# The leftover queries of a batch pair: a feed-forward block of their own instead of a shared block of three tiles

## The chip, the cores and the metric

The kernel runs on one core of one Trainium2 chip, in one launch. The metric is device time in microseconds (us), the median of several executions. A profile is one further execution taken by the hardware profiler; its times are compared with its own execution's time.

The engines are named as in the profile: PE (TensorE, matmuls; PEld its weight loads), DVE (VectorE), ACT (ScalarE), POOL (GpSimd), SP (SyncE, which issues most DMAs).

## The reference

All of attention is float32; the feed-forward weights come as float64.

```
# B, H, S, D = 8, 8, 576, 64
scores = q @ k.T / sqrt(D)                       # per batch and head: 576 x 576
kth    = 32nd largest of each row
scores = where(scores >= kth, scores, -1e9)
attn   = softmax(scores) ; a = attn @ v          # (B, H, S, D)
x      = a.transpose(0, 2, 1, 3).reshape(4608, 512)
h      = x @ w_in                                # 512 -> 2048
g      = where(h > 0, h, exp(min(h, 0)) - 1)     # ELU
out    = g @ w_out                               # 2048 -> 512
```

## The kernel before

**Attention in steps.** The 576 queries of a batch are four tiles of 128 and a rest of 64. A step is one query tile with two heads; a rest step takes 64 queries with four heads, so that it too fills 128 rows. Batches are worked through in pairs, 36 steps a pair, 144 in all. In an even batch the order is tiles (0, 1), tiles (2, 3), rest; in an odd batch it is rest, (4, 5), (6, 7), where 4 to 7 are the odd batch's four tiles. The rests of both batches of a pair lie next to each other and make up one tile of 128 tokens, number 8, which the code calls `rest`. In the first batch of all, tiles go singly.

A step runs through all engines: `scores` multiplies queries and keys on PE (`scps`, line 331), and ACT copies the scaled scores to `sc` (339); `select` finds the 32 largest of each row on DVE, in four rounds of MAX8 and three of MATCH_REPLACE8 for each of two rows of 576; `mask` makes masked exponentials and their sums on ACT (407, 408); `normalise` divides on POOL (418 to 425); `turn` transposes the attention nine times 128x128 on PE (`eps`, 444) and copies it to `et` on ACT (445); `attend` multiplies by the values (`avps`, 470), for two steps at a time where tiles go in twos, and `finish` copies the result to the block's `xT` (497).

**Feed-forward in blocks.** Tiles of tokens are gathered in blocks. When all tiles of a block have their attention, `finish` puts the block's pieces at the end of the list `ffn`. A block has 16 pieces `hidden(f)`, four matmuls each with as many columns as the block has tokens (`hps`, 545), and four pieces `project(s, part)` for each of its tiles, four matmuls each of 512 columns (`ops`, 573). Each float32 matmul of these stands in the profile as two records. After `hidden` ACT takes two Relus (555, 558) out of PSUM whenever a PSUM bank's share is full, `bank = dm // n_tok` pieces: every four pieces for one tile, every two for two tiles, every one for three. Then it takes an exponential (560) and mostly a subtraction of one (564) over `unit = max(2, bank)` pieces; the two halves of the ELU are added on POOL (515) or DVE (517). `project` waits for that sum, and its result goes through `osb` (582) to the output by SP's queue (585).

Pair 0 has the blocks (0), (1), (2), (3), (8), (4, 5), (6, 7). The others have (0, 1), (2, 3), (8, 4, 5), (6, 7). A block of one tile takes its `xT` from `xpool` (three buffers of 128 tokens); a larger one from the pool `xt` (two buffers of `T` tokens). `T` also sizes the buffers of `g` and `n`.

**Who goes when.** After the first eight steps every engine's order is written out by the Python loop (`manual_schedule`). In iteration n it emits `scores` of step n + 2, `attend` of what is closed, `select` of step n in four parts, `mask` of n - 1, `turn` of n - 2 and `normalise` of n - 1, and between them four calls of `feed`. These hand out feed-forward pieces by costs in units of the table `HIDDEN` (per `hidden` piece, by tiles in the block) and `PROJECT`. Each block has a place in the list `due`: the step count at which it is ready, and the cost of all blocks that are ready before it.

```
tiles[qt].block.ready = n + 1.0 if n <= tight else n + 2.5
...
due.append((blk.ready, total))
total += NF * HIDDEN[blk.slots] + 4 * blk.slots * PROJECT
...
ahead = [(w - fed["sum"]) / (x - fed["at"]) for x, w in due if x > fed["at"]]
if ahead:
    fed["over"] += max(0.0, share * min(ahead))
```

So the rate at any time is the smallest over all blocks still to come of (work that must go before the block) / (steps until it is ready). A piece is given out while half its cost is covered by what has gathered in `over`. What is left when the loop ends is emitted in one go, the last pair's block (6, 7) above all.

Of the kernel before, what the change touches and what calls it, by code (L numbers as in the profile page):

```python
# [17 lines left out]
TAKEN = -1.0e30  # L18
EPS = 1.0e-9
STEEP = 2.0**96  # L20
HIDDEN = {1: 1.1, 2: 1.85, 3: 2.7}
PROJECT = 3.55


# [57 lines left out]
def kernel(  # L82
# [10 lines left out]
    P = nc.NUM_PARTITIONS  # L93
# [7 lines left out]
    NC = dm // P  # L101
    NF = dff // P
    NG = NF // 2
    T = 3 * P
    KEYS, QUERIES = R, R + S
    Q = 32
    NB = S // Q
# [383 lines left out]
    def finish(blk, parts, at, cols, src):  # L491
        if blk.xT is None:
            if blk.slots == 1:
                blk.xT = xpool.tile([P, NC, P], FP32, tag="xT", name="xT")
            else:
                blk.xT = late["x"].tile([P, NC, T], FP32, tag="xT", name="xT")
        nc.scalar.copy(blk.xT[:, at, cols], src)
# [23 lines left out]
    def ffn_pieces(blk):  # L521
# [4 lines left out]
        def hidden(f):  # L526
# [3 lines left out]
            elif f % NG == 0 and blk.number > 0:  # L530
                g = late["g"].tile([P, NG, T], FP32, tag="g", name="gT")
                blk.gT.append(g[:])
            if f % unit == 0:
# [4 lines left out]
                else:  # L538
                    n = late["f"].tile([P, 2 * T], FP32, tag="n", name="n")
                blk.n = n[:, 0 : unit * n_tok].rearrange("p (f t) -> p f t", f=unit)  # L540
# [45 lines left out]

        part = HIDDEN[blk.slots]
        behind = 2 * NF if blk.number else 0
# [13 lines left out]
    for b in range(B):  # L602
        if b % 2 == 0:
            rest = 2 * J
            division = [(0,), (1,), (2,), (3,), (rest,), (4, 5), (6, 7)]
            if b > 0:
                division = [(0, 1), (2, 3), (rest, 4, 5), (6, 7)]
            slots = {}
            for part in division:
                blk = Block(len(blocks), len(part))  # L610
                blocks.append(blk)
                slots.update((x, (blk, s)) for s, x in enumerate(part))
        first[b] = len(steps)
        tiles = []
        for qt in range(J + 1):
            r0 = b * S + (JP if qt == J else qt if b == 0 else qt * P)
            if qt == J:
                (blk, slot), c0, n = slots[rest], (b % 2) * R, R
                rows = slice(r0, r0 + R)
            else:  # L620
                (blk, slot), c0, n = slots[(b % 2) * J + qt], 0, P
                rows = slice(r0, r0 + J * (P - 1) + 1, J) if b == 0 else slice(r0, r0 + P)
            c0 += slot * P
            t = Tile(b, qt, rows, blk, slice(c0, c0 + n))
            blk.left += NHP
            blk.tiles[slot].append(t)
            tiles.append(t)
        order = [(0, 1), (2, 3), (J,)] if b % 2 == 0 else [(J,), (0, 1), (2, 3)]
        if b == 0:
            order[:2] = [(0,), (1,), (2,), (3,)]  # L630
        for qts in order:
            for hp in range(NHP // 2 if qts == (J,) else NHP):
                group = Group([tiles[qt] for qt in qts], hp)
                steps += [Step(tiles[qt], hp, group, i) for i, qt in enumerate(qts)]
            for qt in qts:
                n = len(steps)
                tiles[qt].block.ready = n + 1.0 if n <= tight else n + 2.5
    NS = len(steps)
    total = 0.0
    for blk in sorted(blocks, key=lambda x: x.ready):  # L640
        due.append((blk.ready, total))
        total += NF * HIDDEN[blk.slots] + 4 * blk.slots * PROJECT

# [57 lines left out]
    main, rest, other = slice(0, J), slice(J, J + 1), slice(J + 1, 2 * J + 1)  # L701
# [90 lines left out]
```

## Time and profile before

| what | value |
|---|---|
| time, median of three runs | 1645.8 us (1644.03 to 1645.95) |
| the profiled execution: time, span | 1642.57 us, 1640.8 us |
| mean granted TensorE clock | 0.974 |
| PE busy | 1581.7 us, 96% |
| DVE busy | 1453.4 us, 89% |
| ACT busy | 1187.7 us, 72% |
| POOL busy | 708.7 us, 43% |
| `hps` matmul records of 128, 256, 384 columns | 640, 1408, 384 |
| `ops` matmul records of 512 columns | 1152 |

The span is the time from the first instruction to the last. Busy shares are means over stages: in the first 200 us weights are converted and the clock is partly low, then attention and feed-forward run together, and after some 1520 us selection on DVE is over and feed-forward work remains. A matmul's busy time includes its way through the array, which overlaps the next one, so the price of a matmul in a row of equals is the distance from start to start, not its duration. For the same reason an idle time shown for PE is less than what was lost.

### The profile page before, as it was taken

How to read it: one execution, taken by the hardware profiler on the slowest of the kernel's cores; microseconds unless marked ns; L12 is line 12 of the kernel's file. 1: busy time of each engine (PE TensorE's matmuls, PEld its weight loads, DVE VectorE, ACT ScalarE, POOL GpSimd, SP SyncE). 2: the span in 40 equal slices, each digit the busy share in tenths (PEclk: the TensorE clock that was granted, in tenths of full speed). 3: DMA queues.
4: the chain of work that ended last, by engine and by line, in shares of the span. 5: the costliest groups of instructions: out<-in, count | busy, mean ns of one | idle time of the engine just before them, and what ended most of it. 6: DMA issues, size and time to landing. Idle time of an engine off the chain costs nothing.

```text
span 1640.8 us, 25344 instructions
## 1 busy us (share of the span) xinstructions
PE 1581.7 (96%) x8276; PEld 1011.8 (62%) x8276; DVE 1453.4 (89%) x2981; ACT 1187.7 (72%) x2400; POOL 708.7 (43%) x1534
## 2 busy tenths in 40 slices
PE   4788999999999999999999999999999999999999
PEld 3566777666575757555566666655557575755564
DVE  6987999999999999999999699999999599998000
ACT  6887778778695867778678686868759595958521
POOL 4775445445353534445335353535435353534300
PEclk8579999999999999999999999999999999999999
DMA  7431221012100310012100211012100201000000
GB/s 226 151 128 25 50 40 26 7 22 45 42 1 7 59 42 8 7 22 44 36 14 15 43 30 28 1 28 44 36 14 0 43 1 35 1 13 2 7 13 14
DMA packets 188037, 56.18 MB, mean 34 GB/s; under 512 B 178177, under 2 KB 179201, under 8 KB 187905
## 3 DMA queue, kind: packets, MB, share of 16 engines
q1 hardware_dynamic: 186704, 54.26, 14.1%
q8 instruction: 66, 1.08, 0.3%
q14 instruction: 67, 0.54, 0.1%
q10 hardware_dynamic: 1200, 0.30, 0.1%
HBM read 45.09 MB, written 9.44 MB: 33 GB/s over the span
## 4 chain that ended last, share of the span: by engine, by line
PE 76%; ACT 12%; DVE 7%; POOL 3%; issue 1%; DMA 1%; SPq 0%; ACTq 0%; DVEq 0%; POOLq 0%
PE ops L573 29%; PE hps L545 23%; PE avps L470 10%; PE scps L331 7%; PE eps L444 6%; DVE wk L378 3%; DVE m L385 3%; ACT sc L408 2%; ACT et L445 2%; ACT sc L407 2%; DVE m L373 1%; ACT n L564 1%; ACT n L555 1%; ACT sc L339 1%; ACT n L560 1%
## 5 line engine op out<-in xcount | busy, mean ns | idle before, releaser
L385 DVE MAX8 m<-wk 128x8 f32<-128x576 f32 x816 | 577.9, 752 | 0.3 <-POOL den L406 0.3
L545 PE MATMUL hps<-xT,w_in 128*128 128x256 f32 (+2 forms) x2432 | 545.8, 374 | 0.0
L573 PE MATMUL ops<-w_out,gT 128*128 128x512 f32 x1152 | 523.6, 599 | 0.0
L545 PEld LDWEIGHTS hps<-xT,w_in 128*128 128x128 f32 x2432 | 406.0, 192 | 100.1 <-issue 26.3
L378 DVE MATCH_REPLACE8 wk<-m,wk 128x576 f32<-128x576 f32 x544 | 401.4, 748 | 0.0
L573 PEld LDWEIGHTS ops<-w_out,gT 128*128 128x128 f32 x1152 | 209.0, 190 | 233.9 <-issue 232.8
L418 POOL TENSOR_SCALAR dene<-den 128x2 f32<-128x2 f32 x144 | 32.9, 228 | 686.5 <-ACT sc L408 686.1
L408 ACT ACTIVATE sc<-sc,den 128x576 f32<-128x576 f32 x288 | 223.6, 776 | 65.5 <-POOL den L406 44.2
L407 ACT ACTIVATE sc<-sc,m 128x576 f32<-128x576 f32 x288 | 225.3, 782 | 10.8 <-DVE m L385 10.7
L470 PE MATMUL avps<-et,vT 128*64 128x256 f32 (+2 forms) x2080 | 207.2, 330 | 17.4 <-ACT et L445 17.2
L425 POOL TENSOR_SCALAR sc<-sc,rec 128x576 f32<-128x576 f32 x288 | 213.0, 750 | 15.0 <-POOL rec L423 0.2
L331 PE MATMUL scps<-kqT 64*128 64x288 f32 (+1 forms) x1280 | 206.0, 442 | 13.6 <-ACT kqT L307 9.1
L339 ACT ACTIVATE sc<-scps 128x576 f32<-128x576 f32 x288 | 171.8, 647 | 65.1 <-PE scps L331 65.1
L445 ACT COPY et<-eps 128x512 f32<-128x512 f32 x288 | 164.6, 571 | 73.4 <-PE eps L444 73.4
L378 DVE MATCH_REPLACE8 wk<-m,sc 128x576 f32<-128x576 f32 x272 | 200.6, 748 | 0.0
L373 DVE MAX8 m<-sc 128x8 f32<-128x576 f32 x272 | 191.6, 749 | 8.8 <-ACT sc L339 8.8
L444 PEld LDWEIGHTS eps<-ident,sc 128*128 128x128 f32 x1152 | 144.9, 144 | 87.2 <-issue 52.7
L444 PE MATMUL eps<-ident,sc 128*128 128x128 f32 x1152 | 177.1, 279 | 13.7 <-POOL sc L425 13.7
L470 PEld LDWEIGHTS avps<-et,vT 128*64 128x64 f32 x2080 | 128.5, 142 | 98.8 <-ACT et L445 31.7
L515 POOL TENSOR_TENSOR gT<-n,gT 128x512 f32<-128x512 f32 (+1 forms) x119 | 164.9, 1386 | 31.2 <-ACT n L564 31.1
L331 PEld LDWEIGHTS scps<-kqT 64*128 64x128 f32 (+1 forms) x1280 | 111.3, 182 | 89.5 <-issue 43.8
L555 ACT ACTIVATE n<-hps 128x512 f32<-128x512 f32 (+1 forms) x156 | 87.3, 559 | 56.8 <-PE hps L545 56.0
(53 smaller groups left out, 1089.6 us busy)
## 6 DMA issues: line engine op xcount, KB each, us to landing
raw<-in_moe_w_in_dram SPq DMA_DIRECT2D x16, 512.0 KB, 6.1
vT<-in_v_dram SPq DMA_DIRECT2D x64, 128.0 KB, 2.5
raw<-in_moe_w_out_dram SPq DMA_DIRECT2D x16, 512.0 KB, 3.6
out_dram<-osb SPq DMA_DIRECT2D x32, 256.0 KB, 2.1
kin<-in_k_dram SPq DMA_DIRECT2D x112, 72.0 KB, 2.5
qin<-in_q_dram SPq DMA_DIRECT2D x112, 72.0 KB, 2.6
kin<-in_k_dram SPq DMA_DIRECT2D x8, 128.0 KB, 4.5
vT<-in_v_dram SPq DMA_DIRECT2D x64, 16.0 KB, 2.2
```

The lines of the kernel that those rows point to most:

```text
L331: nc.tensor.matmul(wide[i][rows, half, 0:HS], kq[part, q0 : q0 + u.t.ql], kq[part, k0 : k0 + HS], start=True, stop=True,)
L373: nc.vector.max(found[i], cur[i])
L378: nc.vector.match_replace(wk[i], found[i], cur[i], TAKEN)
L385: nc.vector.max(found[i], cur[i])
L407: nc.scalar.activation(sc, sc, AF.Prelu, scale=-1.0, bias=low, alpha=1.0 / STEEP)
L408: nc.scalar.activation(sc, sc, AF.Exp, scale=-STEEP, bias=gap, accum_out=u.den[:, i : i + 1])
L425: nc.gpsimd.tensor_scalar(u.sc[:, i, :], u.sc[:, i, :], rec[:, i : i + 1], 1.0, ALU.mult, ALU.mult)
L444: nc.tensor.transpose(ps[:, c * P : (c + 1) * P], sc[:, c0 : c0 + P], ident[:])
L445: nc.scalar.copy(g.et[:, chunks, u.at, :], ps[:, 0 : n * P].rearrange("p (c q) -> p c q", c=n),)
L470: nc.tensor.matmul(ps[i * D : (i + 1) * D, cols], vt[:, 2 * J + i if c == J else i * J + c, :], w, start=(c == 0), stop=(c == J),)
L545: nc.tensor.matmul(blk.h[:, f % bank, :], w_in[:, i, f * P : (f + 1) * P], blk.xT[:, i, 0:n_tok], start=(i == 0), stop=(i == NC - 1),)
L573: nc.tensor.matmul(blk.o[:], blk.gT[f // NG][:, f % NG, s * P : (s + 1) * P], w_out[:, f, :], start=(f == 0), stop=(f == NF - 1),)
```

## The change

The tile of leftover queries (`rest`, number 8) is a block by itself in all pairs, as it was in pair 0; (4, 5) is then a block of two. Three-tile blocks no longer occur, so their entry in `HIDDEN` goes, and `T`, the largest block's tokens, becomes 256. A pair after the first has five blocks instead of four, and all blocks together cost 1066.4 units by the table instead of 1054.4.

```diff
-HIDDEN = {1: 1.1, 2: 1.85, 3: 2.7}
+HIDDEN = {1: 1.1, 2: 1.85}
...
-    T = 3 * P
+    T = 2 * P
...
             division = [(0,), (1,), (2,), (3,), (rest,), (4, 5), (6, 7)]
             if b > 0:
-                division = [(0, 1), (2, 3), (rest, 4, 5), (6, 7)]
+                division = [(0, 1), (2, 3), (rest,), (4, 5), (6, 7)]
```

`due` and the pieces follow from `division`; no other line differs.

## The prediction

> **What bounds the kernel now.** I read the page's busy times and slices first, then busy time by stretch, then TensorE's waits, then its timeline, since the change touches nearly only matmuls.
>
> ```profile
> PE 1581.7 (96%) x8276; PEld 1011.8 (62%) x8276; DVE 1453.4 (89%) x2981; ACT 1187.7 (72%) x2400; POOL 708.7 (43%) x1534
> PE   4788999999999999999999999999999999999999
> DVE  6987999999999999999999699999999599998000
> PEclk8579999999999999999999999999999999999999
> ```
>
> PE and DVE are both full to slice 35; then DVE stops and PE alone goes on. The page cannot say which is late, so I ask for stretches (PE's busy time is the second figure, DVE's the fourth):
>
> ```profile
> 350.00:560.00 210.00, 206.49 (x1041) 135.26 (x1040) 210.00 (x432) 159.44 (x323) 93.36 (x213) 1.00 0.15 30
> 560.00:780.00 220.00, 215.84 (x1145) 133.68 (x1144) 220.00 (x453) 169.63 (x345) 100.62 (x223) 1.00 0.14 27
> 780.00:990.00 210.00, 210.00 (x1084) 131.66 (x1083) 195.77 (x405) 151.57 (x306) 88.89 (x207) 1.00 0.14 28
> ```
>
> From 350 to 780 us DVE never stops and PE idles 3.5 + 4.2 = 7.7 us; from 780 on PE never stops and DVE has to wait. Up to 780 DVE sets the pace, after it PE. PE's waits of 350 to 780 us are nearly one kind, a context matmul that waits for ScalarE's copy of the turned attention (total, times, longest):
>
> ```profile
> PE avps L470 <- ACT et L445: 6.1, 10, 1.2
> ```
>
> These idle times are too small, since matmul ends are modelled. Start to start in the timeline, an undisturbed context group takes 839.74 - 837.43 = 2.31 us, and one that waits 549.31 - 545.83 = 3.48: it lost 1.17 us where the row shows 0.53.
>
> ```profile
> 545.83 0.65 PE L470 MATMUL avps<-et,vT 128*64 128x256 f32 x2
> 547.01 2.37 PE L470 MATMUL avps<-et,vT 128*64 128x256 f32 x18 [0.53 <-ACT et L445]
> 549.31 3.72 PE L545 MATMUL hps<-xT,w_in 128*128 128x256 f32 x16
> ...
> 837.43 2.38 PE L470 MATMUL avps<-et,vT 128*64 128x256 f32 x20
> 839.74 3.70 PE L573 MATMUL ops<-w_out,gT 128*128 128x512 f32 x8
> ```
>
> **The new matmuls.** `hidden` has 64 matmuls a block, two records each. Three pairs have a block of three tiles, so 3 x 128 = 384 records of 384 columns become 384 of 128 and 384 of 256. Their price is the pitch, first start to next group's start:
>
> ```profile
> 262.15 1.06 PE L545 MATMUL hps<-xT,w_in 128*128 128x128 f32 x8
> 263.04 0.60 PE L444 MATMUL eps<-ident,sc 128*128 128x128 f32 x4
> ...
> 843.82 1.89 PE L545 MATMUL hps<-xT,w_in 128*128 128x256 f32 x8
> 845.55 0.60 PE L444 MATMUL eps<-ident,sc 128*128 128x128 f32 x4
> ...
> 1475.40 2.75 PE L545 MATMUL hps<-xT,w_in 128*128 128x384 f32 x8
> 1478.07 1.24 PE L331 MATMUL scps<-kqT 64*128 64x288 f32 x8
> ```
>
> 0.89 / 8 = 111 ns for 128 columns, 1.73 / 8 = 216 for 256. The third, 2.67 / 8 = 334, ends at a score matmul; such a change costs about 0.09 us once (the same form ahead of a transpose, at 1487.63, takes 2.58 / 8 = 323). So 111 + 216 - 323 = 4 ns, at most 5: 384 x 5 = **+1.9 us** on PE. Groups of 16 to 24 at 128 columns reach 117 ns; that end gives 384 x 10 = 3.8 us. `project` keeps its 576 matmuls.
>
> A page states another price. The Trainium skill, "TensorE: Matmul & The Clock Gate", section "Back-to-back issue gap", says that in a stream of weight loads and matmuls 128 columns take about 81 ns and 512 about 131, so a quarter of the columns is far more than a quarter of the time; it speaks against this change. As an estimate from that page, 81/131 of this trace's 429 ns for 512 columns would be 265 ns, the sum would grow by 384 x 154 ns = 59 us, and the kernel would be slower. The 111 ns above contradict it here, and I go by the row.
>
> ScalarE has 32 outputs of 384 columns (0.485 us) and 16 of 768 (0.845) per block, 29.0 us; now 24 of 512 (0.592) and 24 of 512 (0.632), 29.4. GpSimd's eight sums of 768 (1.82) become twelve of 512 (1.28): 14.6 to 15.3. Both lie beside PE (ACT 72%, POOL 43%) and I take nothing; if their cover were gone they would cost 0.4 and 0.7 us a pair. SyncE's loads and stores are the same number; stores move and nobody waits for them. `xpool` gives the single block its own xT, which removes a claim on the two wide ones; no wait on those shows.
>
> **What moves.** This is the larger part. `feed` gives out feed-forward work at the smallest rate at which, for each block, all earlier blocks are done when it is ready. Units come from HIDDEN and PROJECT: two tiles 58.0, one 31.8, three 85.8. Pairs have 36 steps. Following the `due` list:
> - before: block (4,5) of pair 0 is ready at step 30.5 with 159.0 units ahead; the three-tile blocks at 66.5, 102.5, 138.5 with 391.0, 650.8, 910.6; the last at 146.5 with 996.4. The rates are 232/36 = 6.44 units a step to 66.5, 519.6/72 = 7.22 to 138.5, 85.8/8 = 10.7 to the end.
> - after: the single block is ready at 58.5, so three tiles no longer wait for 66.5. The rates are 7.25 to 54.5 (174/24) and about 7.34 from there to the end (675.4/92).
>
> So work leaves the last eight steps and goes to steps 30 to 66, those in which PE idles. The two programs' instruction orders say the same: TensorE's is identical until about step 30; priced by the pitches, the new one has placed 7 us more PE work by step 36, 14 by 44, 22 by 56, keeps a lead of 25 to 30, and gives it back from step 137 (14 at 140, 5 at 143).
>
> **What it is worth.** One unit is (27.6 + 27.6) / 58.0 = 0.95 us, from the last block in the timeline:
>
> ```profile
> 1581.64 27.79 PE L545 MATMUL hps<-xT,w_in 128*128 128x256 f32 x128
> 1609.27 27.63 PE L573 MATMUL ops<-w_out,gT 128*128 128x512 f32 x64
> ```
>
> Counting nine turning transposes a step, PE in full stretches makes 40 steps from the first turning transpose of step 80 (885.5 us) to that of step 120 (1306.4), 10.52 a step: 7.22 x 0.95 = 6.86 feed-forward and 3.66 attention. At 6.44 units a step would be 6.12 + 3.66 = 9.78, close to DVE's 9.64 (a selection every 9.64 us where it is full). Measured from step 36 (431.3) to 64 (714.6): 283.3 / 28 = 10.12. So 0.34 us a step is lost, about 12 us over the 36 steps; doubling the 7.7 us of idle by the example above gives 15. I take 12. At 7.25 units PE needs 6.89 + 3.66 = 10.55, falls 0.9 us a step behind DVE, and after three steps always has work. Those first steps still wait (about 2 us): **-10 us**. Later, attention waits where the three-tile block begins with nothing left to give out, as at 1491.92: that row's group takes 3.70 instead of 2.31 us. Three of those become ordinary places, but more blocks begin just in time: **-1 us**, with 0 and -3 as ends.
>
> The end is covered: before, step 143 is turned on PE at 1567.1, 57 us after its selection begins at 1510; some 20 is the least that the chain of mask, scaling and turning took (steps 16 to 24). With 10.5 against 9.64 us a step from the last place where DVE is held up, a delay near 26 us grows to about 40, still over 20. So what is late next is PE itself.
>
> Sum: 1.9 - 10 - 1 = **-9 us**. The profiled execution took 1642.57 (span 1640.8 and 1.8 around it) and would take 1633.5; it lies 3.2 us under the median of the runs, 1645.8, so the forecast is **1637**.
>
> **Rivals.**
> - Waits only move (0.13). In the new order the first steps of each odd batch, when DVE has just been held up, carry `hidden` and not `project`; ScalarE then has 6.3 us of attention and 4 x 1.2 us of outputs against PE's 10.5. If twelve context groups there pay 0.8 us each as at 545.83 or less, 9.6 of the 11 go: +0.5, 1646. For it: PE's waits are all on ScalarE. Against: at 858 us the same pattern takes 2.32 us, undisturbed.
> - Slower (0.10): ScalarE falls behind in every `hidden` phase. Some 14 phases follow step 36, each with two context groups; at 1.2 us each (545.83) that is 34 us, where 12 + 3 are lost now, so with 1.9 it is +21 at worst. It decides from 15 + 3.3 - 1.9 = 16.4 us, 0.6 us a group. At 879.09 the second group of a full phase takes 2.84, 0.53 more; the first none, so 0.27 on average.
> - Columns priced by weight loading: to end 3.3 us slower the new matmuls would have to cost 11 + 3.3 - 1.9 = 12.4 us more, 12.4 / 384 = 32 ns above 111. No row after 200 us shows it (0.03).
> - The work moves but gives little because step 30 to 66 lost less than worked out (only the 7.7 shown as idle, 2 of it kept): -5, 1641 (0.14). The change doing nothing is excluded by the order.
>
> **How the numbers follow.** Forecast 0.60; its own range, from 1.9 - 13 - 3 (15 lost, 2 kept) to 3.8 - 8 (12 lost, 4 kept, nothing later), is -14 to -4. The 0.2% that can be told from no change is 3.3 us. Faster by more: 0.60 + 0.14 = 0.74; same: the first rival, 0.13; slower: 0.10 + 0.03 = 0.13. The range runs from -14 to just under the first rival's end, with the -5 case inside: 1631 to 1645; the two slower cases stay out.
>
> **What would show it.** PE's idle time between 350 and 780 us should fall from 7.7 to under 3; DVE should wait more there; the 128-column rows of `hidden` should go from 640 to 1024 records at 111 to 117 ns; PE's last eight steps should take 10.5 us each, DVE end later than 1520, PE's tail shrink. Wrong if TensorE's waits on `et` stay above 10 in number there, or the tail shows idle PE before the last block.

## The result, and the profile after

| | median of runs | profiled execution, span |
|---|---|---|
| before | 1645.1 us (1644.0 to 1646.0, 4 runs) | 1642.57, 1640.8 us |
| after | 1667.9 us (1664.2 to 1668.9, 4 runs) | 1667.47, 1665.7 us |

The changed kernel is slower: ratio 1.0135, 95% interval 1.0117 to 1.0152, some 22 us. The forecast was 1637, faster.

The page of after, the busy times and DVE's slices:

```profile
PE 1584.3 (95%) x8660; PEld 1054.9 (63%) x8660; DVE 1454.5 (87%) x2981; ACT 1191.5 (72%) x2400; POOL 713.1 (43%) x1546
DVE  6988999999999799999998599999998879999400
```

PE has 384 records more and is busy 2.6 us longer, DVE's and ACT's work is nearly the same (1.1 and 3.8 us more), and the span grows by 24.9 us. So engines wait more; none has noticeably more to do. DVE stops a slice later. The same stretches as before (PE's busy time is the second figure, DVE's the fourth):

```profile
350.00:560.00 210.00, 204.29 (x1007) 136.10 (x1009) 200.22 (x412) 156.86 (x314) 90.59 (x200) 1.00 0.14 27
560.00:780.00 220.00, 215.00 (x1264) 142.41 (x1256) 218.96 (x451) 161.03 (x326) 96.55 (x218) 1.00 0.15 29
780.00:990.00 210.00, 204.80 (x993) 128.77 (x992) 178.91 (x368) 149.49 (x299) 87.11 (x198) 1.00 0.13 26
```

PE idles 5.7 + 5.0 us up to 780, where under 3 was forecast, and 5.2 in the stretch to 990 that had none. DVE waits too: neither engine is kept full. PE's waits in total, how often and the longest, up to 780 us and from there on:

```profile
PE avps L470 <- ACT et L445: 10.6, 9, 1.8
...
PE avps L470 <- ACT et L445: 21.1, 16, 2.7
```

It is the same wait as before, context matmuls (those with the values, `avps`) for ScalarE's copy to `et`. Before it was 6.1 us up to 780 us, and from there on:

```profile
PE avps L470 <- ACT et L445: 1.7, 3, 0.8
```

Here is one of these waits in PE's timeline of after, with the block's first pieces:

```profile
740.59 0.60 PE L444 MATMUL eps<-ident,sc 128*128 128x128 f32 x4
741.03 1.89 PE L545 MATMUL hps<-xT,w_in 128*128 128x256 f32 x8
...
753.28 0.65 PE L470 MATMUL avps<-et,vT 128*64 128x256 f32 x2
754.89 2.37 PE L470 MATMUL avps<-et,vT 128*64 128x256 f32 x18 [0.96 <-ACT et L445]
757.20 3.72 PE L545 MATMUL hps<-xT,w_in 128*128 128x256 f32 x16
```

The group takes 757.20 - 753.28 = 3.92 us instead of 2.31. ScalarE's timeline of after tells what it did before that copy:

```profile
752.13 0.57 ACT L555 ACTIVATE n<-hps 128x512 f32<-128x512 f32 x1
752.60 0.58 ACT L558 ACTIVATE gT<-hps 128x512 f32<-128x512 f32 x1
753.08 0.62 ACT L560 ACTIVATE n<-n 128x512 f32<-128x512 f32 x1
753.74 0.63 ACT L564 ACTIVATE n<-n 128x512 f32<-128x512 f32 x1
754.27 0.57 ACT L445 COPY et<-eps 128x512 f32<-128x512 f32 x1
```

Four outputs of `hidden` ("outputs" are from here on the instructions with which ScalarE takes a `hidden` result out of PSUM and makes the ELU's halves) stand ahead of it and take 754.27 - 752.13 = 2.14 us. In the kernel before, in the stretch from which the forecast took its price, the copy stands ahead of them (ScalarE's timeline of before):

```profile
857.64 0.56 ACT L445 COPY et<-eps 128x512 f32<-128x512 f32 x1
858.11 0.59 ACT L555 ACTIVATE n<-hps 128x512 f32<-128x512 f32 x1
```

**Where the order comes from.** A block of two tiles makes outputs after every second piece. While `hidden` pieces are given out, an iteration has four of them at this rate: two by the first two feeds, one by the third, one by the fourth. `turn(done, other)`, with its copy, is emitted between the third and the fourth. As four is a multiple of two, the place of a block's first piece settles on which side of the copy the outputs fall, for as long as an iteration has four pieces. Before, at 843.82 us, the first piece fell in the third feed and the pair was complete in the fourth, behind the copy. After, at 741.03, the first piece falls in the fourth, so pairs are complete in the third, ahead of the copy. The new `due` list moved most blocks to the second place: of the two-tile blocks that begin behind 350 us, without the last, all ten began in the third feed before; after, ten of thirteen begin in the fourth. Where the rate is lower, as before up to step 66 (6.44 / 1.85 = 3.5 pieces an iteration), the side changes within a block. So the block that begins at 532.58 us before, in the third feed too, has outputs ahead of the copy at 545.83.

**How much.** A context group is the run of context matmuls between other work of PE. I took each of the 64 after 350 us, its time to the next group's start less the usual time of its kind (and what the score matmuls just ahead of it took over theirs), and sorted by whether outputs stand directly ahead of the last copy that it waits for ("behind outputs"). The sums move by some 2 us with what is taken as usual; a sum below zero means a little faster than usual:

| kernel | groups behind outputs | they lose | the other groups lose |
|---|---|---|---|
| before | 11 | 11.3 us | 53: 10.4 us |
| after | 26 | 46.9 us | 38: -1.3 us |

Over all of PE's work after 350 us the same reckoning gives 24.5 us lost before and 48.1 after: 23.6 more, with the forecast 1.9 of the columns 25.5, against the span's 24.9.

### The profile page after: what moved, and what is told of

The parts are those of the page before. It is cut to its first block, busy times and chain, and to the rows that moved or that the text cites. A ratio compares the mean times of both kernels' runs of the same rounds, so it can differ in the third digit from the quotient of the medians.

```text
span 1665.7 us, 26171 instructions
## 1 busy us (share of the span) xinstructions
PE 1584.3 (95%) x8660; PEld 1054.9 (63%) x8660; DVE 1454.5 (87%) x2981; ACT 1191.5 (72%) x2400; POOL 713.1 (43%) x1546
## 4 chain that ended last, share of the span: by engine, by line
PE 62%; ACT 25%; DVE 8%; POOL 2%; issue 2%; DMA 1%; SPq 0%; ACTq 0%; DVEq 0%; POOLq 0%
PE ops L573 27%; PE hps L545 14%; PE avps L470 9%; PE scps L331 6%; ACT sc L408 5%; PE eps L444 4%; ACT sc L407 4%; DVE wk L378 3%; ACT et L445 3%; ACT n L564 3%; DVE m L385 3%; ACT n L560 3%; ACT n L555 3%; ACT gT L558 2%; ACT sc L339 1%
## 5 line engine op out<-in xcount | busy, mean ns | idle before, releaser
L385 DVE MAX8 m<-wk 128x8 f32<-128x576 f32 x816 | 619.2, 853 | 3.0 <-POOL den L406 3.0
L545 PE MATMUL hps<-xT,w_in 128*128 128x256 f32 (+1 forms) x2816 | 550.2, 346 | 0.5 <-ACT gT L558 0.5
L545 PEld LDWEIGHTS hps<-xT,w_in 128*128 128x128 f32 x2816 | 451.3, 192 | 65.5 <-issue 23.7
L378 DVE MATCH_REPLACE8 wk<-m,wk 128x576 f32<-128x576 f32 x544 | 428.7, 849 | 0.0
L373 DVE MAX8 m<-sc 128x8 f32<-128x576 f32 x272 | 205.2, 847 | 27.9 <-ACT sc L339 27.8
L515 POOL TENSOR_TENSOR gT<-n,gT 128x512 f32<-128x512 f32 x131 | 167.4, 1278 | 139.8 <-ACT n L564 139.7
L378 DVE MATCH_REPLACE8 wk<-m,sc 128x576 f32<-128x576 f32 x272 | 213.6, 844 | 0.0
L555 ACT ACTIVATE n<-hps 128x512 f32<-128x512 f32 x144 | 85.1, 591 | 79.1 <-PE hps L545 78.9
```

Of the source, the lines that this page charges most:

```text
L373: nc.vector.max(found[i], cur[i])
L378: nc.vector.match_replace(wk[i], found[i], cur[i], TAKEN)
L385: nc.vector.max(found[i], cur[i])
L545: nc.tensor.matmul(blk.h[:, f % bank, :], w_in[:, i, f * P : (f + 1) * P], blk.xT[:, i, 0:n_tok], start=(i == 0), stop=(i == NC - 1),)
```

## Experiments

Theory "place": outputs ahead of the copy cost 1.8 us a group, and the change moved them there. Rivals: "pace", the higher rate overloads ScalarE whatever the order; "columns", the narrow matmuls cost more than their pitch. Counts in the expectations are over the whole program's order; the trace's, after 350 us, are smaller (26 for 27, in one run 30 for 36). The kernel before ran again beside each group, with a median of 1641.3 to 1641.6 us on those chips, so kernels are compared by ratios or within one group.

### Outputs behind the copy, in the changed kernel

```diff
-    feed(n, 0.25)
+    holding[0] = True
+    feed(n, 0.25)                    # third feed: outputs are kept in a list
     if done:
         turn(done, other)
+    holding[0] = False
+    let_go()                         # and emitted here
```

The diff is shortened: in all of it `hidden` puts its outputs into the list `held`. `project` empties the list first, since it needs the sums.

> The changed kernel, with one thing moved: outputs of hidden pieces given out by the third feed of an iteration are emitted behind the copy of the last four turned chunks to et, not ahead of it. Only ScalarE's order (and that of the sums after it) changes; the matmuls and their order stay. Theory 'place': 26 context groups after 350 us have their copy behind such outputs and lose 46.9 us together (1.8 each), the 38 others nothing; so 1667.9 - 46.9 = about 1621, 1618 to 1628. Rival 'pace': the higher rate of feed-forward pieces in steps 30 to 137 overloads ScalarE whatever the order; then the waits return at other places and the time stays above 1655. Rival 'columns': the 128-column matmuls cost more than their pitch; the time stays near 1668.

Measured: 1621.0 us (1617.5 to 1623.0), ratio to before 0.9876 (0.9855 to 0.9897). All of PE's waits after 350 us on other engines, and one stretch, of this kernel:

```profile
PE avps L470 <- ACT et L445: 0.6, 1, 0.6
```

```profile
350.00:560.00 210.00, 210.00 (x1070) 142.96 (x1069) 206.39 (x426) 164.80 (x331) 96.36 (x211) 1.00 0.15 30
```

One copy with its context group, from the timelines of ScalarE and PE of this kernel: the copy now comes first (L565 is line 555 of the others), and the group takes 742.45 - 740.14 = 2.31 us.

```profile
738.99 0.56 ACT L445 COPY et<-eps 128x512 f32<-128x512 f32 x1
739.45 0.60 ACT L565 ACTIVATE n<-hps 128x512 f32<-128x512 f32 x1
...
740.14 2.38 PE L470 MATMUL avps<-et,vT 128*64 128x256 f32 x20
742.45 3.72 PE L550 MATMUL hps<-xT,w_in 128*128 128x256 f32 x16
```

The edit leaves the matmuls and their order as in after; 31.7 us of wait became 0.6, and PE is full. By ratios the move is worth 2.6%, about 43 us, where 46.9 were expected; that 1621 was met to the microsecond is luck, since the time before was 4 us lower on this chip. "Pace" and "columns" both fall: at this pace and with these columns the kernel is faster than before.

### The same in the kernel before

> The kernel before with the same move of outputs behind the copy to et. Theory 'place': 11 context groups stand behind outputs and lose 11.3 us, the 53 others lose 10.4 us for another reason (TensorE waits for VectorE's pace there); so 1645.1 - 11 = 1634, 1629 to 1639, and the change by itself, both with the move, is worth 1621 - 1634 = -13. Rival 'pace': ScalarE is not overloaded at this rate, the order does nothing: 1643 to 1647, and the changed kernel with the move stays slower than this one.

Measured: 1633.7 us (1631.9 to 1636.6), ratio 0.9956 (0.9938 to 0.9974). No group stands behind outputs any more, the others lose 15.5 us, mostly up to 780 us, in the stretch where VectorE sets the pace. The ratio is 7 us of gain; 11 were expected, and the forecast 1634 was met only because this chip's time before was lower. In the reckoning the groups lost 21.7 us (11.3 + 10.4) and still lose 15.5, so part of what was won came back as waits of other groups.

### The copy behind the outputs, in the kernel before

```diff
-    turn(done, other)
+    later = []
+    turn(done, other, later)         # transposes here, the copy kept in the list
...
     feed(n, 0.25)                    # fourth feed
+    for copy in later:
+        copy()
```

> The kernel before, with the copy of the last four turned chunks to et emitted behind the fourth feed and not ahead of it: outputs of pieces that the fourth feed gives out now go first. Matmuls, their order, pace and blocks are those of before. Counted in ScalarE's order, 36 context groups then have their copy directly behind outputs, 12 before. Theory 'place': 24 more at 1.5 to 1.8 us: 1645 + 36 to 43 = 1681 to 1688, with some less where VectorE's pace hides it: 1672 to 1690. Rivals 'pace' and 'columns': both are those of before, so 1643 to 1650.

Measured: 1698.7 us (1697.5 to 1710.3), ratio 1.0368 (1.0331 to 1.0405), beyond the range. With blocks, pace and matmuls of before, the order on ScalarE alone makes the kernel slower than after. PE's waits for the copy after 350 us, 7.8 us before (6.1 + 1.7):

```profile
PE avps L474 <- ACT et L445: 48.7, 34, 2.5
```

In its trace 30 groups, not 36, stand behind outputs and lose 77.9 us, 2.6 each and not 1.5 to 1.8. Its profiled execution is the slowest of its runs (1710.3), and part of the surplus is the clock (last section).

### Other places by a constant, in both kernels

```diff
-    while ffn and decoded[0] >= ffn[0][1] and 0.5 * ffn[0][0] <= fed["over"]:
+    while ffn and decoded[0] >= ffn[0][1] and 0.8 * ffn[0][0] <= fed["over"]:
```

> The changed kernel with one constant: a piece is given out when 0.8 of its cost has gathered, not 0.5. The rate and the blocks stay; pieces fall a little later, in other places of the iteration. Counted in ScalarE's order, 16 context groups have their copy directly behind outputs instead of 27. Theory 'place': 11 fewer at 1.8 us, 1668 - 20 = 1648, 1640 to 1656. Rivals 'pace' and 'columns': rate and matmuls are unchanged, so 1664 to 1670.

Measured: 1647.0 us (1646.3 to 1648.1), ratio 1.0039 (1.0024 to 1.0053). In the trace 15 groups stand behind outputs and lose 25.3 us, the other 49 lose 1.1. No order was written out for this; one constant moved pieces among feeds, and by ratios (1.0135 to 1.0039) some 16 of the 22 us went that the change had cost. 20 were expected; here too the time before was lower on this chip, which brought the result nearer to 1648.

With 0.2 in the kernel before:

> The kernel before with one constant: a piece is given out when 0.2 of its cost has gathered, not 0.5. Rate, blocks and matmuls stay; pieces fall a little earlier, in other places of the iteration. Counted in ScalarE's order, 20 context groups have their copy directly behind outputs instead of 12. Theory 'place': 8 more at 1.0 to 1.8 us, some 8 to 14 us slower: ratio 1.005 to 1.009. Theories in which the blocks or the rate decide: 1.000, 0.998 to 1.002.

Measured: 1665.1 us (1664.4 to 1665.9), ratio 1.0143 (1.0123 to 1.0162). The direction is that of "place", the size is not: 19 groups behind outputs lose 35.3 us, 1.86 each, and the others 8.6. I had priced eight more groups and left the old ones as they were in the kernel before, where they lost 1.0 each; three now lose over 4 us, with the clock halved beside them. This kernel, with the blocks and the rate of before, is as slow as the changed one.

### Half of the move

Against the kernel of the first experiment, shortened:

```diff
-    held.append(lambda n=blk.n, h=blk.h: outputs(f, g, end, n, h))
+    relus(f, g, end, blk.n, blk.h)                  # 555, 558: at once
+    held.append(lambda n=blk.n: outputs(f, g, end, n))   # 560, 564
```

> The changed kernel with half of the move: of the four output instructions of a piece in the third feed, the exponential (560) and the subtraction (564) go behind the copy to et, the two Relus (555, 558) stay ahead of it. By ScalarE's timeline of the changed kernel the moved two take 1.19 of 2.14 us, start to start. Theory 'the copy waits for the time of what is ahead of it': each of the 26 groups loses 1.19 us less, 1.8 - 1.2 = 0.6, 16 us in all instead of 47: 1620 + 16 = 1636, 1630 to 1643. Rival 'the copy waits because the Relus ahead of it wait for the hidden matmuls': the Relus stay, so nothing or little is won, 1655 to 1670.

Measured: 1635.4 us (1633.4 to 1637.9), ratio 0.9966 (0.9954 to 0.9977). PE's waits for the copy after 350 us:

```profile
PE avps L470 <- ACT et L445: 5.4, 12, 1.5
```

All context groups together lose 14 us, where they lost 46.9 - 1.3 = 45.6 in after. So the copy waits for the time of what is ahead of it in ScalarE's queue, not for something that the Relus wait for.

### What the pace and the columns are worth alone

The changed kernel with outputs late, and with the single block's due time put to the step at which the block of three was ready:

```diff
     tiles[qt].block.ready = n + 1.0 if n <= tight else n + 2.5
+    if qt == J and b > 2 and b % 2:
+        tiles[qt].block.ready += NHP * 2
```

> The changed kernel with outputs behind the copy to et, and with the single block of each later pair put into the list of due times at the step at which the block of three was ready, 66.5, 102.5 and 138.5: blocks of one and two tiles at nearly the old pace (6.44 units a step to step 66, then 7.33, 11.2 in the last eight steps). Against the kernel before with outputs late it differs by the 384 records of 128 columns; against the changed kernel with outputs late by the pace. Theory: columns cost their pitch, +1.9 us, and the gain is the pace's: 2 us over the kernel before with outputs late (range -1 to +5) and 11 to 13 over the changed one with outputs late. Rival: the split itself saves (its outputs or its own xT buffer): equal to the changed kernel with outputs late. Rival 'columns' (32 ns more than the pitch each): 14 us over the kernel before with outputs late.

> The kernel before with outputs behind the copy to et, beside the one with the old due times: 0.995 of the kernel before, 0.993 to 0.998, as measured the first time.

> The changed kernel with outputs behind the copy to et, beside the other two: 0.988 of the kernel before, 0.985 to 0.990, as measured the first time.

Measured, on one chip: 1633.5 us with the old due times (0.9954, 0.9940 to 0.9968), 1633.6 for the kernel before with outputs late (0.9953, 0.9937 to 0.9968), 1618.6 for the changed one with outputs late (0.9862, 0.9844 to 0.9879). So the split at the old pace shows no difference (0.1 us), and the new pace is worth 15 us. The 1.9 us of the columns can't be seen, and would not be: the intervals are over 2 us wide to each side, and PE's loss in the trace with the old due times is 11.8 us, against 16.8 in the kernel before with outputs late. The rival of 14 us for the columns is excluded.

The changed kernel with outputs behind the copy is faster than both kernels, by 1.2 to 1.4% against the one before.

## Why the prediction was wrong

**The step that failed** is the one on later waits, "-1 us, with 0 and -3 as ends", together with the price in the "Slower" rival: 0.27 us a group, from the rows at 858 and 879 us. Both rows are of one block, which begins in the third feed (843.82), so that outputs fall behind the copy. I took them for what `hidden` phases cost and didn't ask which of the two orders a block would have after the change, though ScalarE's order of both programs was there to be counted: 12 such groups before, 27 after. The row at 545.83, which lost 1.17 us, has outputs ahead of its copy; I put it down to VectorE's pace. The rival's worst case, +21 us at 1.2 us a group, is close to what happened (+22), but by luck: the runs showed 46.9 us (26 groups at 1.8) for its 34, and for its 15 they showed 23.0: 11.7 won in the other groups and 11.3 that groups behind outputs had lost before. Its mechanism was wrong in one thing: ScalarE does not fall behind for lack of time. With the same work in another order nothing waits.

**Columns, +1.9 us:** not contradicted. The pitch is as taken; in PE's timeline of after, 1.79 / 16 = 112 ns:

```profile
696.54 1.95 PE L545 MATMUL hps<-xT,w_in 128*128 128x128 f32 x16
698.33 0.60 PE L444 MATMUL eps<-ident,sc 128*128 128x128 f32 x4
```

The 265 ns estimated from "TensorE: Matmul & The Clock Gate", section "Back-to-back issue gap", do not hold here; +59 us would have put the version at the old pace near 1692 us; it took 1633.5.

**Work moved to steps 30 to 66, -10 us:** right in kind, and if anything too small. In after, groups without outputs ahead lose nothing (-1.3 us) where they lost 10.4; between the two kernels with outputs late the pace is worth 15 us. It was hidden by the 35.6 us that the groups behind outputs lost in addition.

**ScalarE's outputs, "I take nothing":** right for their amount (1187.7 and 1191.5 us busy), wrong for their place. That is where cover was claimed from a share of 72%: an idle share tells nothing of an instruction that stands behind others in a queue.

**The end is covered:** PE made steps 136 to 143 in 73.0 us, 10.4 each, as forecast, and DVE ended later. But a group there has no score matmuls in front of it to hide the copy, and lost most of all (last section).

**The rival "waits only move":** the waits did return on ScalarE, but in most `hidden` phases, not at the odd batches' first steps alone.

**The signs:** most came although the kernel was slower. DVE waits more up to 780 us, the 128-column records are 1024, the last steps take 10.4 us, DVE ends later (1561 us), and the waits for `et` up to 780 us are 9, under the ten that would have spoken against it. Only PE's idle time there went the wrong way. The number of waits told nothing of their length: nine took 10.6 us where ten had taken 6.1, and the sign did not look behind 780 us, where 16 more took 21.1.

## What to carry to other kernels

When the order of a queue is written by a planner, a change of costs or due times also moves which instruction stands ahead of which; count, in both programs' order, what stands directly ahead of the instruction that the bound engine waits for. Emit the copy that the bound engine waits for ahead of outputs that nobody needs soon, whatever the planner does: this alone was worth some 43 us in the changed kernel (ratios 1.0135 and 0.9876) and only 7 in the other, and it decided which division looked better. A price for a repeated pattern should come from rows of both of its possible orders, or carry both as bounds.

## What was not expected of the hardware

Some waits of PE of 1.9 us and more are followed by a stretch, mostly of 3.4 us, in which half of the clock is granted. In after, PE's timeline and the busy times by stretch (granted clock third from the end):

```profile
1557.05 0.65 PE L470 MATMUL avps<-et,vT 128*64 128x256 f32 x2
1560.42 3.81 PE L470 MATMUL avps<-et,vT 128*64 128x256 f32 x18 [2.73 <-ACT et L445]
1564.16 3.72 PE L545 MATMUL hps<-xT,w_in 128*128 128x256 f32 x16
```

```profile
1560.00:1563.40 3.40, 2.98 (x14) 1.72 (x16) 0.91 (x2) 0.37 (x1) 2.81 (x5) 0.50 0.00 0
1563.40:1567.00 3.60, 3.60 (x19) 2.80 (x16) 0.00 (x0) 1.12 (x3) 0.00 (x0) 1.00 0.00 0
```

The group cost 7.11 us instead of 2.31: 2.73 of shown idle time, and 18 matmuls at half speed. Waits of 0.96 and 1.54 us had no such stretch. The kernel with the copy behind the outputs has eight such stretches of 3.4 us between 350 and 1640 us; at half speed each costs, as an estimate from the granted clock alone, up to 1.7 us, so up to 14 of the 24 us that its groups lost beyond 30 x 1.8 = 54. Over the eleven traces kept, between 350 us and the end of the work, the length of the wait alone does not settle it: of 33 idle times of PE of 1.2 to 1.83 us none was followed by such a stretch, of 17 of 1.93 to 2.73 us twelve were, and one of 2.46 us was not. What else decides is open.
